# GpSimd's fills behind its first weight transfers, and a price for changing TensorE's mode in a list schedule

## The chip, the core and the metric

One core of a Trainium2 chip runs the whole kernel in one launch. The metric is device time in microseconds, the median over runs. TensorE (PE) multiplies matrices into PSUM, VectorE (DVE) and ScalarE (ACT) do the element-wise work, GpSimd (POOL) fills constants and issues the weight transfers, SyncE (SP) issues most other transfers. Each engine works through its own instructions in the order in which the program holds them.

## What is computed

A gated linear recurrence (4 batches, 8 heads, 768 steps, head size 48) is followed by a SwiGLU network on its 3072 rows of 384. Inputs are float32, but the three weight matrices come as 64-bit floats, and the kernel narrows them itself.

```python
mag = sqrt(a_re*a_re + a_im*a_im); scale = minimum(mag, 0.999) / (mag + 1e-6)
for t in range(S):
    new_re = ar*S_re - ai*S_im
    new_im = ar*S_im + ai*S_re
    S_re, S_im = new_re + k[t] (x) v[t], new_im
    y[t] = q[t] @ S_re
xn = x / sqrt(mean(x*x) + 1e-6) * rms_g          # x: the y of all heads, one row per step
out = (silu(xn @ w_gate) * (xn @ w_val)) @ w_out  # 384 -> 1536 -> 384
```

## The kernel before, in words

The sequence is cut into 24 chunks of 128 steps (`N`, `C`). The recurrence is done chunk by chunk in `attend` (line 1078), the network for two chunks at a time, a group of 256 rows, in `feed` (line 1198).

For a unit of one or two chunks, `gates` (line 990) turns the gates into running products of magnitudes and running sums of angles (scans on DVE; roots, arctan and sines on ACT) and multiplies q and k by them (tile `kin`). The result `rot` goes through six SP transfers per chunk into `kq`, with another layout.

A chunk's products on PE are, by their tiles: the scores (`bank<-kq`, 32 calls), two times four transposes of k (`bank<-ident,kq`), the chunk's output (`bank<-am,ve` and `bank<-kq,state`), the update of the state (`bank<-vn,kt`), the sum of squares of the norm (`bank<-ones,sq`), and the spreading of the inverse root over the partitions (`bank<-ident,rs`). After that, DVE writes the normalised columns `xT`, and the group's network may start. Scores, output and update use a quarter of the array's columns per product, four products side by side (96\*32 and 128\*32 in the profile); they are called grouped here. All others, the network's too (`bank<-xT,wg`, `bank<-xT,wv`, then `bank<-wo,hT`, `bank<-sums,hT`, `bank<-hT`), use the whole array. A float32 call makes two instructions in the trace, so the scores' 32 calls are x64 there.

Weights: twelve pieces of 1.5 MB or 768 KB, each fetched on POOL's queue by `fetch` and narrowed by `narrow` (lines 885 and 906). ACT scales the low words (`wo<-wo` or `hT<-hT`), and DVE makes a shift, a combination and an integer addition (`wg<-wo`, `wg<-wo,wg`, and CUSTOM_DVE on `wg<-wo,wg`). POOL reads one word of each landed piece (`junk`). The first two transfers wait for such a read of unit 0's `in_a_im` (line 978); piece 3 waits for a read of chunk 0's `kq` (`seen`). A place in `wo` or `hT` is used again only after the narrowing of what lay there.

The order on every engine is found when the program is built, by the list scheduler `Flow`. Each step is added with an engine, a guessed duration and its tiles (`add`, line 519). `dates` (line 530) gives each a due time, backwards from its users; the products of the network have due times of their own, from a running clock. `schedule` (line 550) plays the engines forward with the guessed durations and takes, wherever an engine is free, the ready step with the earliest due time. `issue` (line 645) writes the result; so almost all instructions carry line 648, and tiles tell them apart. A changed duration or due time can thus reorder any engine, SP's and POOL's queues among them.

At the start (lines 840 to 860) POOL fills constants, the padding columns of the `ve` and `state` tiles, the identity, the mask `causal` (a fill and eight `affine_select`), and the two `am` tiles. None of these steps has a due time except the one that its users give.

Of the kernel before, what the change touches and what calls it, by code (L numbers as in the profile page):

```python
# [19 lines left out]
C = 128  # L20
BLK = 32
# [440 lines left out]
class Flow:  # L462
# [6 lines left out]
    SYNC = 0.12  # L469
    LAND = 2.0  # L470
    LANES = 8
    BEGIN = {"SP": 0.8, "ACT": 0.8, "POOL": 0.8}
    TABLES = {"silu": ("S",), "sin": ("S", "T"), "arctan": ("T",), "rsqrt": ("A",)}

# [41 lines left out]
        kept.append((op["i"], write, p0, p1, lo, hi))  # L516
        self.seen[name] = kept

    def add(self, eng, calls, dur, reads=(), writes=(), table=None, land=None, due=None, after=(), behind=()):
        op = dict(i=len(self.ops), eng=eng, calls=calls, dur=dur, deps=set(), table=table, land=land,  # L520
                  base=due, stage=self.stage, behind={o["i"] for o in behind})
        self.ops.append(op)
        op["deps"].update(o["i"] for o in after)
        for ap in reads:
            self.note(op, ap, False)
        for ap in writes:
            self.note(op, ap, True)
        return op

    def dates(self):  # L530
        users = [[] for _ in self.ops]
        self.next = [[] for _ in self.ops]
        for op in self.ops:
            op["behind"] -= op["deps"]
            for d in op["deps"]:
                users[d].append(op["i"])
            for d in op["behind"]:
                self.next[d].append(op["i"])
        for op in reversed(self.ops):
            due = op["base"] if op["base"] is not None else 1e6  # L540
            for u in users[op["i"]]:
                x = self.ops[u]
                stretch = 1.0 if x["eng"] == "PE" else 1.35
                due = min(due, x["due"] - x["dur"] * stretch - (x["land"] or 0.0) - 0.2)
            op["due"] = due
        for op in self.ops:
            op["due"] += self.shift.get(op["stage"], 0.0)
        return users

    def schedule(self):  # L550
        users = self.dates()
        left = [len(op["deps"]) + len(op["behind"]) for op in self.ops]
        ready = [0.0] * len(self.ops)
        free = {}
        waiting = {}
        table = None
        for op in self.ops:
            free.setdefault(op["eng"], self.BEGIN.get(op["eng"], 0.0))
            waiting.setdefault(op["eng"], [])
            if not left[op["i"]]:  # L560
                waiting[op["eng"]].append(op)
        lanes = {}
        sent = []
        recent = []
        now = 0.0
        order = 0

        def release(o, end, users=users):
            for u in users[o["i"]]:
                x = self.ops[u]  # L570
                lat = self.SYNC if x["eng"] != o["eng"] or o["land"] is not None else 0.0
                ready[u] = max(ready[u], end + lat)
                left[u] -= 1
                if not left[u]:
                    waiting[x["eng"]].append(x)

        def flows(t):
            busy = [q for q in lanes.values() if q]
            whole = sum(q[0][1]["packet"] for q in busy)
            for q in busy:  # L580
                q[0][0] -= (t - now) * q[0][1]["packet"] / whole

        while True:
            best = None
            for eng, ops in waiting.items():
                if ops:
                    t = max(free[eng], min(ready[o["i"]] for o in ops))
                    if eng == "SP" and len(sent) >= self.LANES:
                        if "landed" not in sent[-self.LANES]:
                            continue  # L590
                        t = max(t, sent[-self.LANES]["landed"])
                    if best is None or t < best[0]:
                        best = (t, eng)
            busy = [q for q in lanes.values() if q]
            if busy:
                whole = sum(q[0][1]["packet"] for q in busy)
                q = min(busy, key=lambda q: q[0][0] / q[0][1]["packet"])
                t = now + max(0.0, q[0][0]) * whole / q[0][1]["packet"]
                if best is None or t <= best[0]:
                    flows(t)  # L600
                    now = max(now, t)
                    o = q.pop(0)[1]
                    o["landed"] = now + self.LAND + (1.5 if o["eng"] == "POOL" else 0.0)
                    release(o, o["landed"])
                    continue
            if best is None:
                break
            t, eng = best
            pick = None
            for o in waiting[eng]:  # L610
                if ready[o["i"]] > t + 1e-9:
                    continue
                key = o["due"]
                if o["table"] and table not in self.TABLES[o["table"]]:
                    key += self.switch
                if pick is None or key < pick[0]:
                    pick = (key, o)
            o = pick[1]
            waiting[eng].remove(o)
            dur = o["dur"]  # L620
            if o["table"] and table not in self.TABLES[o["table"]]:
                table = self.TABLES[o["table"]][-1]
                dur += 1.3
                self.loads = getattr(self, "loads", 0) + 1
            if eng == "PE":
                busy = sum(min(e, t) - max(b, t - 4.0) for b, e in recent if e > t - 4.0)
                if busy < 2.0:
                    dur += min(dur, 3.0)
                recent.append((t, t + dur))
                del recent[:-12]  # L630
            o["start"], o["end"], o["order"] = t, t + dur, order
            order += 1
            free[eng] = t + dur
            release(o, t + dur, self.next)
            if o["land"] is not None:
                flows(t)
                now = max(now, t)
                if eng != "POOL":
                    sent.append(o)
                lanes.setdefault(eng, []).append([o["load"] + 0.05, o])  # L640
            else:
                release(o, t + dur)
        assert order == len(self.ops)
# [7 lines left out]
def fast(tc, ctx, qT, kT, v, a_re, a_im, w_gate, w_val, w_out, rms_g, out, H, bad):  # L651

    nc = tc.nc
    B, DM, S = a_re.shape
    D = DM // H
# [7 lines left out]
    HH = H // 2  # L663
# [35 lines left out]
    add = flow.add  # L699
# [39 lines left out]
    def fill(o, x, eng="POOL", **kw):  # L739
        e = nc.vector if eng == "DVE" else nc.gpsimd  # L740
        return add(eng, [(e.memset, (o, x), {})], 0.1 + 0.8e-3 * cols(o), [], [o], **kw)
# [45 lines left out]
    def mm_time(n, m=P):  # L787
        return 2 * max(0.84e-3 * n, 0.83e-3 * m)
# [55 lines left out]
    for t, x in ((ones, 1.0), (halfpi, PI / 2), (mid, -(RE_MAX + RE_MIN) / 2),  # L844
                 (width, -(RE_MAX - RE_MIN) / 2), (mhalf, -0.5), (zeros, 0.0)):
        fill(t, x)
    for t in ves + states:
        fill(t[:, :, :, D:], 0.0)
    add("POOL", [(make_identity, (nc, ident), {})], 0.6, [], [ident])
    fill(causal, 1.0)  # L850
    for e in range(2):
        for b in range(4):
            x = causal[b * BLK:(b + 1) * BLK, e]
            add("POOL", [(nc.gpsimd.affine_select, (), dict(out=x, in_=x, pattern=[[1, C]],
                                                            compare_op=ALU.is_ge, fill=0.0,
                                                            base=-BLK * (3 - b if e else b),
                                                            channel_multiplier=-1))], 0.3, [x], [x])
    for t in ams:
        fill(t, 0.0)
    for t in banks[4:6]:  # L860
        fill(t, 0.0, eng="DVE")
    dma(gcol, rms_g.rearrange("(c p) -> p c", p=P))
# [81 lines left out]
    turn = {}  # L944
# [133 lines left out]
    def attend(n):  # L1078
# [12 lines left out]
        for a in range(2):  # L1091
# [3 lines left out]
            for h in range(HH):  # L1095
                for b in range(4):
                    c = 3 - b if h % 2 else b
                    list_.append((s[c * BLK:(c + 1) * BLK, h, b * BLK:], k[:, a * HH + h, b * BLK:(b + 1) * BLK],
                                  q[:, a * HH + h, b * BLK:], True, True))
            mms(list_, HH // 2 * 0.29, due=EARLY.get(n))  # L1100
            pairs = lambda t: t.rearrange("s (m e) t -> s m e t", e=2)
            mask = causal.bitcast(I32).unsqueeze(1).to_broadcast([C, HH // 2, 2, C])
            o = am[:, a * HH:(a + 1) * HH]
# [17 lines left out]
            for x, (l_, r_) in enumerate(todo):  # L1121
                lines[c].append((o, l_, r_, x == 0, x == len(todo) - 1))
        order = [lines[c][i] for i in range(len(lines[0])) for c in range(4)]
        mms(order, len(order) * mm_time(C) / 4 * 1.1 + 0.15)
        if not last:
            kt = kts[0]
            for a in range(2):
# [6 lines left out]
            ps = banks[5][0:D2, 0:DM]  # L1134
            st = ps.rearrange("p (h d) -> p h d", h=H)
            mms([(st[c * BLK:(c + 1) * BLK, h], kt[:, h, c * BLK:(c + 1) * BLK], vv[:, h], True, True)
                 for h in range(H) for c in range(3)], H * 0.1)
            st4 = ps.rearrange("p (m e d) -> p m e d", m=NP, e=2)
            u, i = unit_of[n], n - UNITS[unit_of[n]][0]
            decay = decays[way_of(u)][:, :, i].rearrange("p (m e) -> p m e", e=2).unsqueeze(3).to_broadcast([D2, NP, 2, D])  # L1140
# [156 lines left out]
    o = 0  # L1297
# [68 lines left out]
```

## Time and profile before

| what | us |
|---|---|
| median of 3 runs (lowest, highest) | 734.04 (733.62, 735.03) |
| the profiled execution, its own time | 735.44 |
| its span in the profile | 733.7 |
| PE busy in the span | 679.7 |
| DVE, ACT, POOL busy | 473.2, 331.3, 42.0 |
| mean granted PE clock | 0.984 |

A row of the profile's timeline has the start in us, the length, the engine, the line, the operation, out<-in, the shape and a count; in brackets stands how long the engine was idle before it and what ended that. A merged row's length goes from the first start to the last end, and matmuls overlap: the distance between two starts is what a stretch of products takes. The kernel has two parts: up to about 60 us the first chunks and weights are prepared and PE mostly waits; from there PE is almost always busy.

### The profile page before, as it was taken

The numbers are of one execution on the slowest core, as the hardware profiler recorded it, in microseconds if no ns is written. First come the engines' busy times: TensorE is split into PE (matmuls) and PEld (weight loads), VectorE is DVE, ScalarE is ACT, GpSimd is POOL, SyncE is SP. The second block draws the span as 40 slices with busy tenths as digits, with TensorE's granted clock in tenths as the row PEclk, the third lists the DMA queues.
The fourth block names the chain that finished last, engine by engine and source line by source line (L and its number), as shares of the span: only waits on it lengthen the run. The fifth ranks groups of instructions, "written<-read, shape, count | busy, mean of one in ns | idle before, by whom it ended". The sixth has DMA issues, their size and how long they took to land.

```text
span 733.7 us, 16076 instructions
## 1 busy us (share of the span) xinstructions
PE 679.7 (93%) x6842; PEld 598.6 (82%) x6842; DVE 473.2 (64%) x740; ACT 331.3 (45%) x451; POOL 42.0 (6%) x80
## 2 busy tenths in 40 slices
PE   0269989999999999999999999999999999999996
PEld 0257866877888889889889889889889889889885
DVE  6979897789798887886856745765845233234121
ACT  7646856867384742841832732731830110111010
POOL 5122200000000000000000001000000000000000
PEclk9978999999999999999999999999999999999999
DMA  8597675544756625643523303313303202200000
GB/s 296 186 318 211 163 178 160 140 128 110 195 129 152 177 84 139 215 145 78 151 66 77 119 22 73 113 34 79 106 1 77 66 13 67 65 12 3 22 0 27
DMA packets 104575, 80.64 MB, mean 110 GB/s; under 512 B 42800, under 2 KB 95280, under 8 KB 104496
## 3 DMA queue, kind: packets, MB, share of 16 engines
q1 hardware_dynamic: 100432, 64.99, 33.2%
q0 software_dynamic: 3264, 14.16, 5.6%
q8 instruction: 56, 0.92, 0.5%
q10 hardware_dynamic: 800, 0.39, 0.2%
q14 instruction: 23, 0.19, 0.1%
HBM read 55.84 MB, written 4.72 MB: 83 GB/s over the span
## 4 chain that ended last, share of the span: by engine, by line
PE 64%; DVE 2%; DMA 2%; SPq 2%; ACT 1%; issue 0%; DVEq 0%; ACTq 0%
PE bank L648 64%; SPq L648 2%; DMA kq<-rot 1%; DMA in<-in_a_im_dram 1%; DVE turns L648 0%; DVE t L648 0%; ACT turns L648 0%; DVE hT L648 0%; DVE large L648 0%; DVE xT L648 0%; DVE in L648 0%; ACT L648 0%; DVE small L648 0%; DVE ot L648 0%; DVE rot L648 0%
## 5 line engine op out<-in xcount | busy, mean ns | idle before, releaser
L648 PE MATMUL bank<-xT,wg 128*128 128x256 f32 x864 | 200.8, 382 | 2.8 <-DVE xT L648 2.8
L648 PE MATMUL bank<-xT,wv 128*128 128x256 f32 x864 | 199.0, 380 | 0.0
L648 PEld LDWEIGHTS bank<-xT,wg 128*128 128x128 f32 x864 | 164.4, 191 | 25.9 <-DVE xT L648 3.5
L648 PEld LDWEIGHTS bank<-xT,wv 128*128 128x128 f32 x864 | 163.6, 190 | 22.5
L648 PE MATMUL bank<-wo,hT 128*128 128x192 f32 (+1 forms) x576 | 124.8, 360 | 0.5 <-DVE hT L648 0.4
L648 DVE TENSOR_TENSOR hT<-bank,sg 128x512 f32<-128x512 f32 x72 | 49.4, 687 | 108.6 <-PE bank L648 104.9
L648 PEld LDWEIGHTS bank<-wo,hT 128*128 128x128 f32 x576 | 94.6, 190 | 14.2 <-issue 1.4
L648 ACT ACTIVATE sg<-bank 128x512 f32<-128x512 f32 x72 | 42.8, 595 | 133.3 <-PE bank L648 132.9
L648 ACT ACT_TABLE_LOAD x68 | 87.2, 1283 | 16.3 <-DVE rot L648 8.6
L648 PE MATMUL bank<-kq 96*32 96x96 f32 (+3 forms) x1536 | 35.5, 243 | 33.8 <-DVE wg L648 28.2
L648 PEld LDWEIGHTS bank<-kq 96*32 96x32 f32 x1536 | 31.7, 114 | 39.7 <-DVE wg L648 28.2
L648 DVE TENSOR_TENSOR rot<-kin,turns 128x768 f32<-128x768 f32 x48 | 44.9, 953 | 18.4 <-DMA kq<-rot 17.5
L648 ACT ACTIVATE sq<-bank 128x384 f32<-128x384 f32 x24 | 11.7, 487 | 96.5 <-PE bank L648 95.8
L648 POOL TENSOR_TENSOR rs<-ssv,mhalf 128x1 f32<-128x1 f32 x24 | 18.4, 766 | 573.1 <-DVE ssv L648 573.1
L648 ACT ACTIVATE kt<-bank 128x384 f32<-128x384 f32 x40 | 18.4, 486 | 64.4 <-PE bank L648 63.6
L648 PE MATMUL bank<-sums,hT 128*128 128x192 f32 x240 | 45.2, 330 | 0.0
L648 PE MATMUL bank<-am,ve 128*32 128x128 f32 x768 | 41.4, 290 | 0.4 <-DMA ve<-in_v_dram 0.4
L648 PEld LDWEIGHTS bank<-sums,hT 128*128 128x128 f32 x240 | 39.4, 190 | 0.4 <-DVE mid L648 0.3
L648 DVE TENSOR_TENSOR hT<-hT 128x768 f32<-128x768 f32 x40 | 38.2, 954 | 0.9
L648 DVE COPY_PREDICATED am<-causal,bank 128x512 f32<-128x512 int32 x48 | 32.9, 720 | 8.1 <-PE bank L648 8.1
L648 ACT ACTIVATE turns<-in 128x768 f32<-128x768 f32 (+1 forms) x39 | 29.9, 789 | 14.8 <-DVE in L648 11.0
L648 PE MATMUL bank<-kq,state 96*32 96x128 f32 x640 | 35.6, 285 | 0.0
(110 smaller groups left out, 715.6 us busy)
## 6 DMA issues: line engine op xcount, KB each, us to landing
kq<-rot SPq DMA_DIRECT2D x144, 128.0 KB, 2.4
kin<-in_q_dram SPq DMA_DIRECT2D x24, 192.0 KB, 3.1
kin<-in_k_dram SPq DMA_DIRECT2D x24, 192.0 KB, 4.4
wo<-in_w_gate_dram SPq DMA_DIRECT2D x6, 768.0 KB, 4.4
out_dram<-ot SPq DMA_DIRECT2D x24, 192.0 KB, 2.2
wo<-in_w_val_dram SPq DMA_DIRECT2D x6, 768.0 KB, 5.0
wo<-in_w_out_dram SPq DMA_DIRECT2D x6, 768.0 KB, 4.7
in<-in_a_re_dram SPq DMA_DIRECT2D x11, 384.0 KB, 4.5
```

The source lines that it names most:

```text
L648: fn(*args, **kw)
```

## The change

There are two edits, both in what the scheduler is told. First, a step can carry a `late` time, before which it is not due. It is set to 12 (the scheduler's us) on the fills of padding, the identity, the mask with its eight selections, and the `am` fills. Second, a PE step can carry a `mode`. The three grouped kinds get one; whenever the mode changes along PE, the scheduler adds 0.06 us to that step's guess. The guesses of the grouped steps are lowered (0.29 to 0.285 for each pair of heads in the scores; the factor 1.1 and the constant 0.15 of the output to a factor of 1.06). The attribute `turn`, a bias in the choice for staying in a mode, is 0.0. No instruction is added or removed by the text of the diff.

```diff
+    turn = 0.0
...
-    def add(self, eng, calls, dur, reads=(), writes=(), table=None, land=None, due=None, after=(), behind=()):
+    def add(self, eng, calls, dur, reads=(), writes=(), table=None, land=None, due=None, after=(), behind=(), late=None, mode=None):
...
             op["due"] += self.shift.get(op["stage"], 0.0)
+            if op["late"] is not None:
+                op["due"] = max(op["due"], op["late"])
...
+                if eng == "PE" and o["mode"] != mode:
+                    key += self.turn
...
+            if eng == "PE" and o["mode"] != mode:
+                mode = o["mode"]
+                dur += 0.06
...
+    LATE = 12.0
     for t in ves + states:
-        fill(t[:, :, :, D:], 0.0)
-    add("POOL", [(make_identity, (nc, ident), {})], 0.6, [], [ident])
-    fill(causal, 1.0)
+        fill(t[:, :, :, D:], 0.0, late=LATE)
+    add("POOL", [(make_identity, (nc, ident), {})], 0.6, [], [ident], late=LATE)
+    fill(causal, 1.0, late=LATE)
...
-                                                            channel_multiplier=-1))], 0.3, [x], [x])
+                                                            channel_multiplier=-1))], 0.3, [x], [x], late=LATE)
     for t in ams:
-        fill(t, 0.0)
+        fill(t, 0.0, late=LATE)
...
-            mms(list_, HH // 2 * 0.29, due=EARLY.get(n))
+            mms(list_, HH // 2 * 0.285, due=EARLY.get(n), mode=BLK)
...
-        mms(order, len(order) * mm_time(C) / 4 * 1.1 + 0.15)
+        mms(order, len(order) * mm_time(C) / 4 * 1.06, mode=BLK)
...
-                 for h in range(H) for c in range(3)], H * 0.1)
+                 for h in range(H) for c in range(3)], H * 0.1, mode=BLK)
```

More of the change, by code (lines that the diff above doesn't have):

```diff
@@ L517, in note @@
         self.seen[name] = kept
-    def add(self, eng, calls, dur, reads=(), writes=(), table=None, land=None, due=None, after=(), behind=()):
+    def add(self, eng, calls, dur, reads=(), writes=(), table=None, land=None, due=None, after=(), behind=(), late=None, mode=None):
         op = dict(i=len(self.ops), eng=eng, calls=calls, dur=dur, deps=set(), table=table, land=land,
-                  base=due, stage=self.stage, behind={o["i"] for o in behind})
+                  base=due, late=late, mode=mode, stage=self.stage, behind={o["i"] for o in behind})
         self.ops.append(op)
@@ L556, in schedule @@
         table = None
+        mode = None
         for op in self.ops:
```

## The prediction

> **What bounds the kernel now.** I read the page first, then the chain of waits, then PE's timeline for every row with idle time before it.
>
> ```profile
> span 733.7 us, 16076 instructions
> ...
> PE 679.7 (93%) x6842; PEld 598.6 (82%) x6842; DVE 473.2 (64%) x740; ACT 331.3 (45%) x451; POOL 42.0 (6%) x80
> ...
> PE 64%; DVE 2%; DMA 2%; SPq 2%; ACT 1%; issue 0%; DVEq 0%; ACTq 0%
> ```
>
> PE is idle for 733.7 - 679.7 = 54.0 us. Its timeline tells where:
>
> ```profile
> 28.22 2.36 PE L648 MATMUL bank<-kq 96*32 96x128 f32 x64 [28.22 <-DVE wg L648]
> ...
> 43.96 2.36 PE L648 MATMUL bank<-kq 96*32 96x128 f32 x64 [4.78 <-DMA kq<-rot]
> ...
> 58.65 4.49 PE L648 MATMUL bank<-xT,wg 128*128 128x256 f32 x12
> 62.97 2.75 PE L648 MATMUL bank<-xT,wv 128*128 128x256 f32 x12
> ...
> 98.01 1.33 PE L648 MATMUL bank<-kq 96*32 96x128 f32 x64 [0.82 <-DMA kq<-rot]
> 101.83 0.55 PE L648 MATMUL bank<-ident,kq 96*128 96x96 f32 x4 [2.01 <-DVE am L648]
> 125.39 2.86 PE L648 MATMUL bank<-xT,wg 128*128 128x256 f32 x12 [0.65 <-DVE xT L648]
> ...
> 237.87 0.54 PE L648 MATMUL bank<-vn,kt 128*32 128x48 f32 x24 [1.65 <-ACT kt L648]
> ...
> 351.18 2.86 PE L648 MATMUL bank<-xT,wg 128*128 128x256 f32 x12 [0.98 <-DVE xT L648]
> ```
>
> About 39 us lie before the first network product at 58.65. After it the stalls are 0.82, 2.01, 0.65, 0.33 (at 183.01), 1.65, 0.98, 0.89 (681.30), 0.41 (723.12): 7.7 us, and some 6 us after PE's last product. So the time moves with the start of the network at 58.65, with these stalls, and with what PE's own order costs. I then laid the changed kernel's order on each engine beside the old one; PE's products are the same in number.
>
> **POOL's part.** Before, the first weight transfer starts here:
>
> ```profile
> 2.39 2.28 POOL L648 TENSOR_SCALAR_AFFINE_SELECT causal<-causal 32x128 f32<-32x128 f32 x7
> 4.73 0.17 POOL L648 COPY junk<-in 1x1 f32<-1x1 f32 x1
> ...
> 6.09 0.91 POOL L648 DMA_DIRECT2D wo<-in_w_gate_dram  x1
> ...
> 8.54 1.46 DVE L648 TENSOR_SCALAR t<-t 128x384 f32<-128x384 f32 x1
> ```
>
> In the new order only four of the eight selections pass behind the two transfers; identity, one state fill, mask fill and one `am` fill stay ahead. Four at 2.28/7 = 0.33 make 1.3 us: the transfers start at about 4.8, and the first piece lands at 13.6, where `junk` saw it at 14.94. Directly this buys nothing: DVE takes the piece at 25.41 and ACT at 19.94, long after. What moved behind is hidden too: the mask is read first at 33.79.
>
> One rule is to be weighed. SBUF — State Buffer, section "Who interferes with whom", has GpSimd and a DVE `tensor_scalar` in its fast mode exclude each other for a whole instruction. The row at 8.54 fits: 1.46 us, against 0.33 for its like at 11.08, and it ends with POOL's last fill at 10.04. If the fills were gone by then, 1.1 us would be won on the gates; were they pushed later, more would be lost. But POOL has no gap from 0.8 to 10.04 and does the same instructions in any order, so its last fill ends at about 10.0 again. I take 0; the ends are -0.5 and +0.5.
>
> **DVE and ACT up to the first network product.** Since the scheduler now believes the weights to be early, DVE gets piece 0's shift and combination (0.94 + 1.76) between 18.0 and 20.7, where it had idled 1.59 us waiting for ACT's sines, and ACT gets `wo<-wo` (1.60) before those sines in place of an `in,mid` step (0.60). The sines end 1.0 later, at 21.0; DVE, with a displaced `kin` product (0.55), is ready at 21.1. So `turns` and `rot` of chunk 0 come at 21.1 and 22.1 instead of 20.06 and 21.06: the first scores go from 28.2 to 29.2. For chunk 1, DVE then has the other `kin` product, piece 0's addition, piece 1's shift and combination and half of the mask step first, but no longer piece 0's first two steps: its `rot` starts at 33.25 instead of 32.05, +1.2. Its six SP transfers took until 43.96 on a crowded DMA; I let them keep their length: 45.2. SP also issues one more quarter of `ve` behind them, four instead of three; the last landed at 48.1, now at 49.5 or so. The chunk's output product then ends at 53.4 instead of 51.8. But ACT, which had spent 50.27 to 53.16 on the next unit's roots and a table load, now takes `sq` at once: 53.45 against 53.16. From there to `xT` is the same chain (`kt`, norm, POOL's power, spreading), less a DVE combination that stood before `xT` (56.06 to 57.82). The network starts at about 58.4. The state update (57.22 to 58.65, 1.43) has moved behind the network's first part, so PE has that still to do: 58.4 + 1.4 - 58.65 = **+1.2**. Ends: -0.5 (the `ve` quarter lands with the rest) and +3.5 (DMA more crowded).
>
> **The stalls.** Unit 1's preparation is ahead: piece 4's addition (1.75) is already done when DVE turns to the next unit, and piece 9's two steps (0.56 + 0.96) go behind `rot`. That is 3.3 us off what stands before `kq` of chunk 2, so the wait at 98.01, although only four of the eight `wo,hT` calls now stand before it, should stay under 0.3. At 101.83 PE waits for `am` to free a bank. The new order puts four `wo,hT` calls (2.7 us) between the two sets of transposes, and the `am` steps ahead of about 4.5 us of weight work: 2.01 goes. At 125.39 transposes (0.45) come between spreading and network: 0.65 becomes 0.2. In all 3.48 becomes 0.3: **-3.2**; ends -3.5 and 0.
>
> At 237.87 the second half of the update waits for `kt`, which stands on ACT behind a step that waits 4.67 us for `in_a_im`. In the new order the update comes after that network stage, and spreading, three `sums` calls and transposes (1.7 us) cover `xT`: 1.65 becomes 0.3, **-1.3**; ends -1.65 and 0. At 351.18 half of the scores (0.7) has moved ahead of the spreading, so the cover for `xT` shrinks from 1.26 to 0.7: **+0.3**; ends -1.0 and +0.6. The last group's order is unchanged, so 681.30 and the tail stay.
>
> **PE's changes of mode.** The order has 57 stretches of grouped products before and 60 after. The page names nothing like a switch, so I take distances of starts. Network products following scores start 2.69 apart, otherwise 2.59: 0.10. Scores cut in two (404.74 and 434.12) take 0.70 twice, uncut (220.76 to 222.02) 1.26: 0.14. So a stretch more costs 0.24, three cost **+0.7**. TensorEngine Tiling (Array Packing), section "Key Properties", says that a change of tiling mode drains TensorE; with the 128 cycles of draining of TensorE: Matmul & The Clock Gate, section "Step-by-step: what each phase is for", at its 2.4 GHz, two changes are an estimated 0.11 us, and three stretches 0.3. The rows are measured here, so 0.7 stands; 0.3 is the other end. The rule speaks against this order; the 0.06 of the scheduler avoids nothing.
>
> **Sum.** 1.2 - 3.2 - 1.3 + 0.3 + 0.7 = -2.3. The profiled execution (735.44, span 733.7) would become 733.1 and 731.4; it lies 1.4 above the median, so on the median: 734.04 - 2.3 = 731.7.
>
> **The rivals.** (1) The network starts late, and the result is slower. Chunk 1's `kq` transfers, issued 1.2 later, meet weight pieces that are 1.2 earlier: piece 4's is asked for at 37.9 instead of 39.11. Against it: piece 3 leaves the queue earlier too. For it: these transfers took 7.4 us to land here, but 2.3 for chunk 0 on a quiet DMA. If `kq` or the last `ve` land 4 us later than I take them, the start costs 5.5 instead of 1.2 and the time is 736.0. It decides from where the start term passes 3.5, a network start after about 60.7.
>
> (2) The stalls only move. DVE is 74 to 99% busy in 20 us stretches from 60 to 240, and a PE that arrives earlier finds the next unit unready. If half of the 4.5 comes back later, the sum is about 0: 734.0.
>
> (3) The edits do not do what they say: the weights come earlier, but nobody on the path wants them, and the start follows the old path exactly, as ACT's and DVE's lost time is absorbed in the wait for chunk 1's transfers. With start 0 and the 351.18 stall gone: -3.2 - 1.3 - 1.0 + 0.5 = -5.0, 729.0.
>
> **Chances.** Main case 0.48, (1) 0.20, (2) 0.24, (3) 0.08. The main case's own range is 730.0 to 733.5. Within 0.2% means 732.6 to 735.5, about what a measurement of this kernel can tell from no change. Faster 0.52 (most of the main case, (3)), same 0.27 ((2), and the main case's edge), slower 0.21. The range, 729.2 to 736.0, reaches over (2) and to the middle of (1).
>
> **What would show it.** POOL's first transfer at 4.8; `rot` of chunk 0 at 22.1; first scores at 29.2, second at 45.2; the network's first product at 58.4; no wait above 0.5 between 90 and 126; the update after the network around 237. If the network starts after 60.7, (1) is right; if new waits on `xT`, `kq` or `am` fill 130 to 240, (2); if PE's busy time rises by over 1.5, the price of a mode change is wrong.

## The result, and the profile after

The changed kernel takes 728.18 us (727.07 to 729.33, 4 runs) against 733.83 us for the one before in the same series: a ratio of 0.9917, interval 0.9896 to 0.9937. A later series gave 727.29 (725.70 to 729.46, 5 runs) against 734.38: 0.9900, interval 0.9880 to 0.9920. The prediction was 731.7 with a range down to 729.2; the gain is 6 to 7 us, not 2.3.

The profiled execution took 727.07. The page of the changed kernel:

```profile
span 725.4 us, 16062 instructions
...
PE 677.1 (93%) x6842; PEld 596.2 (82%) x6842; DVE 471.3 (65%) x740; ACT 331.5 (46%) x450; POOL 45.8 (6%) x80
...
PE 88%; DVE 4%; SPq 3%; DMA 2%; issue 1%; ACT 1%; POOL 0%; DVEq 0%; ACTq 0%
```

The chain that ended last is now 88% PE (64% before): it seldom leaves PE. PE's busy time fell by 2.6 us with the same 6842 products, so they ran faster. PE's timeline after, the rows that answer to those of before (start, length, what; in brackets the idle time before it):

```profile
28.47 2.36 PE L657 MATMUL bank<-kq 96*32 96x128 f32 x64 [28.47 <-DVE in L657]
...
44.67 2.36 PE L657 MATMUL bank<-kq 96*32 96x128 f32 x64 [4.34 <-issue]
...
56.30 4.48 PE L657 MATMUL bank<-xT,wg 128*128 128x256 f32 x12 [0.72 <-DVE xT L657]
...
89.20 0.88 PE L657 MATMUL bank<-vn,kt 128*32 128x48 f32 x48
...
92.78 1.33 PE L657 MATMUL bank<-kq 96*32 96x128 f32 x64
...
94.44 2.77 PE L657 MATMUL bank<-wo,hT 128*128 128x384 f32 x8
97.05 0.49 PE L657 MATMUL bank<-ident,kq 96*128 96x96 f32 x4
...
116.83 2.86 PE L657 MATMUL bank<-xT,wg 128*128 128x256 f32 x12 [0.32 <-DVE xT L657]
...
227.66 2.86 PE L657 MATMUL bank<-xT,wg 128*128 128x256 f32 x12
```

A row without brackets had no wait. Of the 7.7 us of waits behind the first network product, 1.6 are left: 0.32 here, 0.89 at 672.72 and 0.41 at 714.55. The four `wo,hT` calls at 94.44 stand where PE used to wait for `am`. The deferred update of the state is the row at 89.20.

The second difference is PE's granted clock. Before, in 2 us windows behind the wait at 101.83 (columns: window, its length, busy us of PE, PEld, DVE, ACT, POOL, PE clock, DMA share, GB/s):

```profile
100.00:102.00 2.00, 0.17 (x2) 0.17 (x3) 2.00 (x5) 1.53 (x3) 0.00 (x0) 1.00 1.10 312
102.00:104.00 2.00, 2.00 (x48) 1.88 (x51) 2.00 (x4) 0.49 (x1) 0.00 (x0) 0.74 1.13 225
104.00:106.00 2.00, 2.00 (x59) 1.99 (x54) 2.00 (x2) 0.53 (x2) 0.00 (x0) 0.50 0.21 21
106.00:108.00 2.00, 2.00 (x66) 1.85 (x59) 1.08 (x3) 1.97 (x5) 0.29 (x1) 0.91 0.21 34
```

The same products after:

```profile
96.00:98.00 2.00, 2.00 (x28) 1.36 (x30) 2.00 (x5) 0.76 (x3) 0.00 (x0) 1.00 0.68 191
98.00:100.00 2.00, 2.00 (x101) 1.98 (x92) 1.78 (x3) 1.29 (x4) 0.00 (x0) 1.00 0.45 105
```

Idle from 99.8 to 101.83, PE ran at half clock from about 103 on, for some 3.4 us (the 1.7 us lost there are half of that): 59 products in a window, against 101. The wait cost 2.0 us and the clock behind it 1.7 more (2 us times one minus the clock, summed over the windows).

To keep such sums apart I read every profile in the same way. A is the start of the sixth and last stretch of `xT,wg` of the first network part; then come the time from A to the end of the span, PE's waits in it, and what low clock took between A and 700 us. The rest is PE's own work and its tail.

| profile | span | A | A to end | waits | low clock | rest |
|---|---|---|---|---|---|---|
| before | 733.7 | 86.28 | 647.4 | 7.7 | 1.7 | 638.0 |
| changed, first profile | 725.4 | 83.92 | 641.5 | 1.6 | 0.0 | 639.9 |
| changed, later series | 727.7 | 86.55 | 641.2 | 2.1 | 0.0 | 639.1 |

So 6 us of the gain lie behind A in both profiles of the changed kernel, although A itself moved by 2.6 between them. But the row of before is one execution. In the profiles of three runs below that keep its order on PE from A on, the same stretch took 644.1 and 646.7 (changed start) and 647.6 (POOL's order alone), so by the profiles the gain behind A is between 2.5 and 6. The rest holds the deferred update, which before stood ahead of A: 0.9 of its rise.

### The profile page after: what moved, and what is told of

Same layout as the page of the kernel before. It is cut to its first block, busy times and chain, and to the rows that moved or that the text cites. A ratio compares the mean times of both kernels' runs of the same rounds, so it can differ in the third digit from the quotient of the medians.

```text
span 725.4 us, 16062 instructions
## 1 busy us (share of the span) xinstructions
PE 677.1 (93%) x6842; PEld 596.2 (82%) x6842; DVE 471.3 (65%) x740; ACT 331.5 (46%) x450; POOL 45.8 (6%) x80
## 4 chain that ended last, share of the span: by engine, by line
PE 88%; DVE 4%; SPq 3%; DMA 2%; issue 1%; ACT 1%; POOL 0%; DVEq 0%; ACTq 0%
PE bank L657 88%; SPq L657 3%; DMA kq<-rot 1%; DVE wg L657 1%; DVE t L657 1%; DMA decay<-ends 1%; DVE turns L657 1%; DMA in<-in_a_re_dram 1%; ACT t L657 0%; ACT L657 0%; POOL rs L657 0%; DVE xT L657 0%; DVE ot L657 0%; DVE am L657 0%; DVE rot L657 0%
## 5 line engine op out<-in xcount | busy, mean ns | idle before, releaser
L657 DVE TENSOR_TENSOR hT<-bank,sg 128x512 f32<-128x512 f32 x72 | 49.5, 688 | 112.7 <-PE bank L657 101.9
L657 PE MATMUL bank<-kq 96*32 96x128 f32 (+3 forms) x1536 | 35.9, 244 | 32.8 <-DVE in L657 28.5
L657 POOL TENSOR_TENSOR rs<-ssv,mhalf 128x1 f32<-128x1 f32 x24 | 20.5, 856 | 575.5 <-DVE ssv L657 575.5
L657 PE MATMUL bank<-am,ve 128*32 128x128 f32 x768 | 38.4, 283 | 0.0
L657 ACT ACTIVATE t<-t 128x768 f32<-128x768 f32 (+1 forms) x39 | 30.8, 791 | 5.5 <-DVE t L657 5.1
```

What stands on the lines that cost most here:

```text
L657: fn(*args, **kw)
```

## The experiments

Theory A: the gain comes from the new order of PE, DVE, ACT and SP around PE's waits, and the fills on POOL as such bring next to nothing. Theory B: the earlier weights bring it by themselves. Theory C: a wait costs more than its length, because low clock follows it; D: it does not. Some kernels run the scheduler twice, with the guesses of before and of the change, and take each engine's order from one of the two (`old`, `new`).

**One edit at a time.** The `late` edit alone, with the guesses of before and no price for the mode:

```diff
-                dur += 0.06
+                dur += 0.0
...
-            mms(list_, HH // 2 * 0.285, due=EARLY.get(n), mode=BLK)
+            mms(list_, HH // 2 * 0.29, due=EARLY.get(n), mode=BLK)
...
-        mms(order, len(order) * mm_time(C) / 4 * 1.06, mode=BLK)
+        mms(order, len(order) * mm_time(C) / 4 * 1.1 + 0.15, mode=BLK)
```

> Only the late time of the fills; guesses and mode as before; the scheduler is free. Theory A (the gain is a better order of PE's products around the waits of 98 to 126 and 237, and what the scheduler was told about the fills is only one of two nudges towards it): some other order comes out; if it still puts products between the two sets of transposes of chunk 2, about 728 to 731, otherwise about 733. Theory B (the fills themselves bring the gain, by the earlier weights and by a DVE step that no longer collides with them): about 728, as in the changed kernel.

Measured: 727.77 (726.18 to 730.47), ratio 0.9904 [0.9880, 0.9928]: the whole gain. Its waits from A on are 3.4 us, and the first of them is 0.32 at 119.52. The second edit alone:

```diff
-    LATE = 12.0
+    LATE = None
```

> Only the mode and the guesses of the grouped products; the fills as before; the scheduler is free. Theory A: between 728 and 733, depending on the order that comes out; with the waits at 98 to 126 gone it is near 729. Theory B: 734, no change, as the fills are where they were.

Measured: 735.70 (733.40 to 736.83), ratio 1.0009 [0.9991, 1.0027]: nothing. Its profile has the old start, and in PE's timeline one wait in the place of another:

```profile
98.68 1.33 PE L657 MATMUL bank<-kq 96*32 96x128 f32 x64 [1.13 <-DMA kq<-rot]
...
106.34 2.36 PE L657 MATMUL bank<-kq 96*32 96x128 f32 x64 [2.12 <-DMA kq<-rot]
```

The wait for `am` is gone, but 2.12 us for `kq` came up, and the scores after it took 2.36 instead of 1.33: half clock again. So removing one wait was not enough.

**Start or network.** The changed order up to the first network product, the old one after it, and the reverse (`front(old, new)`); `first` gives the time of that product:

```diff
+        def front(a, b):
+            t = first(a)
+            out = {}
+            for e in a:
+                head = {i: r for i, s, r in a[e] if s < t}
+                out[e] = list(head.items()) + [(i, 1e6 + r) for i, s, r in b[e] if i not in head]
+            return out
...
+        return front(new, old)
```

> The order of the changed kernel on all engines up to the first network product, and from there the order of before. Theory A: the network starts some 2 earlier (56.5 to 57.5, the state update included before it), but the old order's waits at 98 to 126 and at 237 come back, perhaps shorter: 731 to 733. Theory B: nearly all of the gain, 728 to 729.

> The order of before up to the first network product, and from there the order of the changed kernel. Theory A: the network starts as before (58.5), the waits after it shrink from 7.7 to 2 or 3, and PE does not run at the half clock around 104: 728 to 731. Theory B: 733 to 734.

Measured: changed start 732.27, ratio 0.9976 [0.9957, 0.9995]; changed network part 730.22, ratio 0.9936 [0.9912, 0.9960]. That is -2.0 (interval -3.2 to -0.4) and -4.1 (-6.5 to -2.9), and together about the whole. With the changed start alone, PE's timeline still has the waits:

```profile
96.88 1.33 PE L704 MATMUL bank<-kq 96*32 96x128 f32 x64 [1.19 <-DMA kq<-rot]
100.20 0.55 PE L704 MATMUL bank<-ident,kq 96*128 96x96 f32 x4 [1.51 <-DVE am L704]
```

With the old start and the changed network part they are gone, and A to the end takes 641.6 us, as in the changed kernel, although the first network product comes as late as 59.84:

```profile
59.84 4.76 PE L704 MATMUL bank<-xT,wg 128*128 128x256 f32 x12
```

The larger part of the gain needs no early weight at all. B falls.

**POOL's order alone.** Before's order on four engines, the changed one on POOL:

```diff
+        return {e: [(i, r) for i, s, r in (new if e == "POOL" else old)[e]] for e in old}
```

> The order of before on every engine but POOL; POOL has its instructions in the changed kernel's order (four selections behind the two first weight transfers). It isolates the first edit's own target. Theory A (the gain is the order of PE, DVE, ACT and SP, and POOL's part only takes the collision at DVE's TENSOR_SCALAR away): that row near 8.5 shrinks from 1.46 to about 0.36, the gates come 0.8 earlier, chunk 0's scores about 27.4 instead of 28.2; chunk 1's kq is bound by its transfers, so the network starts between 57.8 and 58.7, all waits after it stay (2.01 at about 101, 1.65 at about 237). Time 0 to -0.8 against before, 733.5 to 734.3. Theory B (weights 1.3 us earlier bring the gain by themselves): network start below 57, time 728 to 730.

Measured: 735.62 (732.02 to 740.68, 12 runs), ratio 1.0029 [1.0005, 1.0053]. DVE's row is short, as in the changed kernel, and the gates come earlier (first scores 27.74), but the time goes up. PE's timeline has new waits at other places:

```profile
164.78 0.84 PE L694 MATMUL bank<-vn,kt 128*32 128x48 f32 x46 [0.64 <-ACT kt L694]
168.64 0.77 PE L694 MATMUL bank<-kq 96*32 96x128 f32 x32 [0.66 <-DVE state L694]
```

The direction was wrong in both expectations. The profiled execution had a span of 733.3, 0.4 below before's, so it doesn't show where the 1.5 us between the medians went; that stays open. The counterpart has the changed start on PE, DVE, ACT and SP, but before's order on POOL:

```diff
+        x = front(new, old)
+        x["POOL"] = [(i, r) for i, s, r in old["POOL"]]
+        return x
```

> The changed kernel's order on PE, DVE, ACT and SP up to the first network product, then before's; POOL has before's order throughout. Beside the run with the same orders and POOL's new order (0.9976 of before) it tells what of the start's gain is POOL's. Theory A: the TENSOR_SCALAR near 8.5 is back at 1.46 and the gates 0.8 later, so half of the start's gain or more goes: -0.5 to -1.3 against before, 733.0 to 733.8. Theory E (the start's gain is all in the order of DVE and PE behind the gates): -2, 732.3. If my prediction's start term had been right for the order alone: +1.2, 735.5.

Measured: 731.92 (729.56 to 735.57, 12 runs), ratio 0.9968 [0.9944, 0.9993]: -2.2, no less than with POOL's new order (-2.0). So theory E holds for the start, and what I had said of A there falls: within the intervals, POOL's part is worth nothing. This kernel is also the cleanest look at my own start steps, since the collision is back (DVE's timeline):

```profile
8.61 1.39 DVE L706 TENSOR_SCALAR t<-t 128x384 f32<-128x384 f32 x1
...
22.05 0.96 DVE L706 TENSOR_TENSOR rot<-kin,turns 128x768 f32<-128x768 f32 x1
...
33.25 1.83 DVE L706 TENSOR_TENSOR rot<-kin,turns 128x768 f32<-128x768 f32 x2
```

`rot` at 22.05 and 33.25, first scores at 29.30: the prediction said 22.1, 33.25 and 29.2. Up to there its steps were right.

**The clock.** Useless products in PE's longest wait, with before's order otherwise:

```diff
+        op["calls"] = list(op["calls"]) + [(nc.tensor.matmul, (banks[b][:, 0:P],), dict(lhsT=ident, rhs=ident, start=True, stop=True))] * count
```

> The order of before, with eight useless whole-array products (ident times ident, 128 columns, about 0.22 us each, 1.7 us in sum, into the output bank that the next products overwrite) put on PE where it waits 2.01 us for am, ahead of the second four transposes of chunk 2. The wait itself stays as long as it was, only PE is busy in it. Theory C (the wait costs more than its length, because PE runs at half clock for about 4.5 us after it): the clock of 102 to 108 goes from 0.74, 0.50, 0.91 to 1.00, the output's stretches from 0.67 to 0.40, the update from 1.42 to 0.88, and the time falls by 1.5 to 2: 732.3 to 732.8. Theory D (the low clock there has another cause, or the lost time is absorbed in a later wait): 734.3, within 0.5.

Measured: 733.21 (731.54 to 734.49, 12 runs), ratio 0.9987 [0.9971, 1.0002]. The profile does what theory C says:

```profile
102.00:104.00 2.00, 2.00 (x64) 1.89 (x68) 2.00 (x4) 0.49 (x1) 0.00 (x0) 1.00 1.07 237
104.00:106.00 2.00, 2.00 (x85) 1.91 (x77) 2.00 (x2) 1.57 (x5) 0.00 (x0) 1.00 0.19 19
106.00:108.00 2.00, 2.00 (x35) 1.41 (x24) 1.62 (x4) 1.97 (x3) 0.56 (x1) 1.00 0.18 28
```

From chunk 2's scores to the next chunk's it now takes 7.66 us (98.08 to 105.74) instead of 9.27 (98.01 to 107.28): -1.6. But the median moved by 0.9, and the interval reaches from -2.1 to +0.1. The same treatment of the waits ahead of the network, in before's order (counts 12 after chunk 0's sum of squares, 6 after chunk 1's, and the 8 above):

> The order of before, with useless products (ident times ident, 128 columns) in its early waits: twelve after chunk 0's sum of squares, six after chunk 1's, and eight in the wait of 2.01 us at 101.83. It asks what the orders are worth when PE's clock is high in both: compare with the changed kernel that was treated alike (726.6). Theory C (some 3 us of the change's 5.7 are PE clock that its order no longer loses): the mean clock goes from 0.987 over the runs of before to 0.993 or more, the time to 730 or 731, and the distance to the treated changed kernel is 3 to 4. Theory D (the clock is no part of the gain): 733 or more, the distance stays at 6.

Measured: 732.74 (729.18 to 740.10, 12 runs), ratio 0.9994 [0.9971, 1.0016]. The mean clock rose from 0.987 to 0.990, less than expected. The time fell by 1.6 between the medians and by 0.4 in the ratio, whose interval reaches from -2.1 to +1.2: it includes D and excludes the 3.4 or more that C asked for. The profiled execution was the quickest of the twelve and says nothing of the median. And in the changed kernel, 9, 8 and 3 products after chunk 0's sum of squares, chunk 1's, and its spreading:

> The changed kernel, with twenty useless whole-array products (ident times ident, 128 columns) put where PE waits before the network: nine after chunk 0's sum of squares (the wait of 4.34 us before chunk 1's scores), eight after chunk 1's sum of squares (2.40) and three after its spreading (0.72). Theory C (half speed follows a wait): chunk 1's scores shrink from 2.36 to about 1.4, the first twelve network products from 4.48 to about 2.75 and the clock of 56 to 60 goes from 0.55 and 0.60 to 1.00; -1.8 to -3 us against the changed kernel, 725 to 726.5. Theory D: 728, or some tenths more, since nine products at half speed (3.9 us) just fill the first wait.

Measured: 726.64 (725.86 to 727.80, 5 runs), ratio 0.9893 [0.9872, 0.9915], 0.7 to 1.5 under the changed kernel's two medians: less than theory C asked for. The network's first twelve products take 2.86 instead of 4.48, but the network starts late (PE's timeline):

```profile
39.57 2.25 PE L657 MATMUL bank<-ident 128*128 128x128 f32 x18
45.36 2.36 PE L657 MATMUL bank<-kq 96*32 96x128 f32 x64 [3.53 <-issue]
...
57.76 2.86 PE L657 MATMUL bank<-xT,wg 128*128 128x256 f32 x12
```

The nine ran at full clock, so were over after 2.25 us, and the idle time behind them was enough for the scores to run at half speed again. Hence fourteen:

> The changed kernel with fourteen useless products after chunk 0's sum of squares, eight after chunk 1's and three after its spreading. With nine in the first place PE was done with them at 41.8 and then idle for 3.5 us, and chunk 1's scores and output still ran at half speed. Theory C: with fourteen the wait shrinks to about 2.5, the half clock after it is rarer or shorter, the network starts at 55.5 to 56.5 instead of 57.8: 725 to 726. If the length of the wait isn't what brings the low clock (theory D), or the products at half speed (6 us) delay chunk 1's scores: 727 to 729.

Measured: 727.01 (724.54 to 728.62, 6 runs), ratio 0.9899 [0.9876, 0.9921]: no better. In PE's timeline the start is as early as hoped, and is lost again much later:

```profile
43.25 1.33 PE L657 MATMUL bank<-kq 96*32 96x128 f32 x64
...
53.99 2.86 PE L657 MATMUL bank<-xT,wg 128*128 128x256 f32 x12
...
505.95 4.54 PE L657 MATMUL bank<-xT,wg 128*128 128x256 f32 x12 [1.43 <-DVE xT L657]
```

Here a wait of 1.43 us (no other profile has more than 0.46 near that place) was followed by twelve products in 4.54 instead of 2.75 us: the wait cost its length and 1.8 more. Last, the `late` edit alone with 10 useless products behind chunk 0's output, 8 behind its sum of squares, 8 behind chunk 1's and 3 behind its spreading:

> The kernel with the first edit alone (727.8), with ten useless products behind chunk 0's output, eight behind its sum of squares, eight behind chunk 1's and three behind its spreading. Same order of the network part as the changed kernel within a few steps, other order of PE at the start. Theory C: 725.5 to 726.5, as the treated changed kernel. Theory D: 727.8.

Measured: 725.01 (724.74 to 725.60, 4 runs), ratio 0.9875 [0.9854, 0.9895], with a mean clock of 0.9975. PE's timeline:

```profile
44.49 1.33 PE L657 MATMUL bank<-kq 96*32 96x128 f32 x64
...
55.02 2.86 PE L657 MATMUL bank<-xT,wg 128*128 128x256 f32 x12
```

It is the fastest kernel here, 2.8 under the same order without these products in the other series (727.77), as theory C expects; the two intervals against before overlap a little ([0.9880, 0.9928] there). Clock and start go together here: without these products the network started at 58.62 in its profile, 3.6 later, and not all of that need be clock, since the issue of chunk 1's last `kq` transfer took 2.33 us there and 0.60 here. On the same chip the changed kernel itself gave:

> The changed kernel itself once more, on the same chip as the treated versions, for its mean clock over many runs: Theory C: 0.991 to 0.993 against 0.987 before, which is 3 us of a 730 us span, and 728 us. Theory D: the same 0.987.

Measured: 727.29 (725.70 to 729.46, 5 runs) with a mean clock of 0.992. The ranges of these two don't overlap, though their intervals against before do. Over 17 to 29 runs in each of the three series before's mean clock was 0.986 or 0.987. The mean clock is weak evidence, though: the changed kernel's two profiles have 0.995 and 0.986, and most of that difference is chunk 1's scores and output, for which the first says 1.00 and the second 0.50 although the scores took 2.36 us in both.

## Why the prediction was too cautious

**The step that failed.** Cut by the medians, most of the miss lies in the start. For the network part the prediction had -3.2 - 1.3 + 0.3 + 0.7 = -3.5, and the run with the old start measured -4.1, with -3.5 inside its interval. For the start it had +1.2, and the two runs with the changed start measured -2.0 and -2.2, with intervals that end below 0. The step that was wrong leads from chunk 1's scores to the end of its output: the last `ve` was to land at 49.5 and the output to end at 53.4. In the changed kernel's first profile the late quarters had landed by 47.7, and in the four profiles with the changed order at the start the output ended at 50.7 to 52.7. The base of the sum was early, too: before's profile has the first network product at 58.65, but the two others with its order up to there have it at 59.84 (the old start, above) and 59.76 (eight useless products in the longest wait). With the changed start it came at 57.38 and 57.62. The second fault, a term put at nothing, is the clock behind a wait; it is plain in the profiles, less so in the medians.

Its terms, for the first pair of profiles (-8.3) and for the changed kernel's second profile (-6.0), in us. The start is A's move plus the deferred update (0.9); the row of the mode is what remains, without that update:

| step | predicted | first profile | second profile |
|---|---|---|---|
| start of the network | +1.2 | -1.5 | +1.2 |
| waits behind it | -4.2 | -6.1 | -5.7 |
| low clock behind A | not in the sum | -1.7 | -1.7 |
| the rest (predicted: changes of mode) | +0.7 | +1.0 | +0.2 |
| sum | -2.3 | -8.3 | -6.0 |

**The missing term: a wait was priced at its length.** The sum took 2.01 us off for the wait at 101.83 and nothing for the clock behind it, although the profile of before showed it: the output's stretches there took 0.67, and later (227.78 to 229.11) 0.40. The clock page of the Trainium skill (TensorE: Matmul & The Clock Gate, section "What's actually happening") says that the array falls back to half rate after an idle window of about 3.4 us. Here 2.01 us of idle time were enough, and at 505.95, in the run with fourteen useless products, 1.43; so the measured rows decide. In the profiles this term is 1.7 us. How much it is in the medians is less sure: filling the waits of before's order brought 0.9, interval -0.1 to 2.1, in one case and 0.4, interval -1.2 to 2.1, in the other.

**Waits: right place, too small.** From 98.01 to 125.39 the prediction had -3.2, and 0.32 of 3.48 is left: right, for the reason given (the four `wo,hT` calls at 94.44). At 351.18 it had +0.3 for a shrinking cover; there is no wait, so -1.0. That step failed: it took the place of DVE's `xT` as fixed and looked only at what PE does ahead of it. It is absent in the second profile and in both with useless products in that order, but there with the `late` edit alone (0.78 at 345.47) and with the old start (0.85 at 345.20). What decides it I didn't test. The 0.33 at 183.01 also went.

**The wait at 237.87 was not the order's.** The sum took 1.3 off for it. None of the three runs that kept before's order on PE (POOL's new order alone, and the two with useless products) had it, nor did the two with the changed start and before's order behind it; one of them has the update in one piece there, 0.94 at 234.24. In before's profile it came behind ACT's wait of 4.67 us for `in_a_im`. The saving was counted in this pair of profiles, but the runs give no sign of it in the median, so that part of the agreement is luck; other waits took such a place in other runs (164.78 and 168.64 above).

**The start: POOL's step was wrong, the next ones right, the last wrong.** "The same instructions in any order, so its last fill ends at about 10.0 again": that argument failed in both halves. The timelines of POOL and DVE in the changed kernel:

```profile
4.54 0.91 POOL L657 DMA_DIRECT2D wo<-in_w_gate_dram  x1
...
6.24 2.40 POOL L657 TENSOR_SCALAR_AFFINE_SELECT causal<-causal 32x128 f32<-32x128 f32 x4
```

```profile
8.51 0.36 DVE L657 TENSOR_SCALAR t<-t 128x384 f32<-128x384 f32 x1
...
21.25 0.96 DVE L657 TENSOR_TENSOR rot<-kin,turns 128x768 f32<-128x768 f32 x1
```

The four selections took 2.40 instead of the 1.3 of their like, POOL ended at 11.1, and yet DVE's instruction was not held: 0.36 instead of 1.46. POOL's order decides that: 0.36 also with POOL's new order alone, 1.39 with the changed start and POOL's old order. In the old one it ran beside a row of fills, in the new one it began in the last of the selections; why this one doesn't hold it isn't shown. My value of 0 should have been -0.8, outside the end of -0.5 that I gave. It is of no use for the time (the runs with POOL's order alone, and without it).

DVE's and ACT's shifts (+1.0 and +1.2) were as predicted, as the run with before's order on POOL shows. The last step, from chunk 1's scores to the network, failed. I had put `ve` 1.4 later, and PE waiting for it. Its four late quarters were issued by 40.8 and landed within 6.9 us, and PE never waits for `ve` in the changed kernel; before, it waited 0.44. So the chunk's output ended at 50.7 in the first profile and 52.7 in the second, not at 53.4. With the update ahead of it, as I had counted, the network would have started at 59.8; the two runs with the changed start have that order, and it started at 57.38 and, with before's order on POOL, here:

```profile
57.62 2.93 PE L706 MATMUL bank<-xT,wg 128*128 128x256 f32 x6
```

The two profiles of the changed kernel differ by 2.6 us in A. Chunk 1's scores began at 44.67 in one and 45.82 in the other, when its transfers had landed, and its output ran mostly at full clock in the one and at half in the other. "I let them keep their length" was wrong as well: the six `kq` transfers took 7.4 us to land before (median), and 7.2 to 8.0 in all six profiles without the changed start, but 3.8 to 5.0 in all eight with it or with the order of the `late` edit alone. What saved the predicted 45.2 is the last of the six, which took 8.0 and 8.7 in the changed kernel's two profiles; where it landed after 5.1, in the first run with the changed start, the scores began at 42.00. So this goes with the order, not with chance alone. A likely reason, not tested, is that weight piece 3 leaves POOL at 29.1 instead of 30.8. I made one sum from one execution, and the start's lower end of -0.5 was too near.

**Mode.** The price of +0.7 for three stretches is compatible with +1.0 and +0.2; the runs can't tell it from the 0.3 of the rule. PE's busy time fell, so the predicted sign of a wrong price did not show.

**The rivals.** The late start (1) did not happen: 56.3 and 58.6, not past 60.7. The moving waits (2) did not come in the changed kernel, but they did when the mode edit or POOL's order was made alone. (3) was nearest in its time, 729.0, and right about 351.18, but wrong in what it rests on: the edits do what they say, with another use. Calling fills late pushed the scheduler to another order, and that order is the gain; on which of PE, DVE, ACT and SP it rests was not separated.

## What to carry to other kernels

Price a PE wait of more than a microsecond by its own length and by the rows that follow it: compare the same products a few hundred us later, and add the difference. Ask of every wait in a profile whether the program's order makes it or one late transfer did; a second profile of the same kernel tells, and a sum from one execution carries its luck. An edit in a list scheduler's due times acts through the order of everything: cut the order by engine and by time to see which part of it pays.

## What the runs showed of the hardware

- The clock column can miss half speed: chunk 1's 64 score products took 2.36 us in the changed kernel's first profile, where the column says 1.00, and 1.33 at 92.78. In the second profile the same products took 2.36 and the column says 0.50. The durations of like products are the safer reading.
- Low clock is not a fixed answer to a wait: 1.51 us for `am` was followed by 1.7 us lost to it with POOL's order alone, and by none with the changed start (A to 700), on about the same products; with that start and POOL's old order, 1.35 us was followed by 1.7 again.
- POOL's selections were slowed from 0.32 to 0.60 each in a row that ran beside two-input products on DVE, and DVE's one-input TENSOR_SCALAR took 1.46 us beside POOL's fills and 0.36 in POOL's new order.
- The time of before's order scatters more (731.6 to 741.0 over 29 runs, and 729.2 to 740.1 over 12 with useless products) than that of the changed order, of which there are fewer runs (725.7 to 729.5 over 9).
